# Hash-masked attention and a two-layer block on one core: a new hand-written order for the first two chunks, and a new place for the value shares

## The chip, the core and the metric

The kernel runs on one core of a Trainium2 chip. Times are device microseconds of one launch of the whole program. The kernel before takes 311.88 us (median of 3 runs, 311.78 to 311.99). A core has five instruction streams that run side by side and wait for each other through semaphores: PE (TensorE, matrix products, with a separate row PEld for weight loads), DVE (VectorE), ACT (ScalarE), POOL (GpSimd) and SP, which here only issues DMAs. Each stream runs its instructions in the order in which the program emitted them, so an instruction that waits holds up all that stand behind it on the same engine.

## The reference

Four batches, 8 heads, 768 positions, head size 64. Queries and keys are hashed to six bits each, a query attends only to keys of its own bucket, and the result goes through a normalised two-layer block with a residual:

```
q_bits = einsum('bhsd,dk->bhsk', q, proj) > 0        # six bits; k_bits likewise
mask   = q_bucket[:, :, :, None] == k_bucket[:, :, None, :]
scores = where(mask, scale * q @ k.T, -1e9)
attn   = softmax(scores)                              # plus 1e-9 in the denominator
x      = (attn @ v).transpose(0, 2, 1, 3).reshape(B, S, H * D)
xn     = (x - mean) / sqrt(var + 1e-6) * g_ln
out    = x + relu(xn @ w_ch1) @ w_ch2                 # 512 -> 2048 -> 512
```

## The kernel before

**Tiling.** The work is cut into 12 chunks of 256 query positions, (batch, third) in order: chunks 0 to 2 are batch 0, chunks 3 to 5 batch 1, and so on. A chunk's attention has 12 units: four pairs of heads, three groups of four key blocks for each pair. `att_units` gives four steps for each unit: `scores` (S, four products into a tile `sc`, two buffers), `exps` (X, one 128x1024 exponential on ACT), `values` (V, eight products into an accumulator `av`) and `divide` (D, after the third group of a pair). The mask is part of the scores' product: six rows of plus or minus one half, one for each hash bit, lie below the 64 rows of each head in the operand tiles `slots`. The accumulator `av` lies in one of two PSUM banks, av0 and av1; chunk 0 uses av0 only, other chunks alternate from pair to pair.

**The block.** `mlp_steps` gives for each chunk the normalisation, eight `up` steps (eight products of 128x256 each into `hp`, then a rectifying copy R by DVE or ACT) and eight `down` steps (four products of 128x512 each). The block of one chunk runs as filler between the attention units of the next.

**Operands.** For batches 1 to 3, the operands are made by POOL casts (`narrow`, N), a DMA transpose issued by SP (`operands`, T), a DMA that shifts every second block (`shifted`, P), DVE block transposes (B), hash products (H), a store of the bits to DRAM and four loads of them as rows (J). For batch 0 this would take too long, so `first_two` builds them on the engines: TensorE transposes of the f32 tiles into a PSUM tile `tpose` (T, or LT for the late thirds), a scaled copy to SBUF (`scaled`, E), casts of its upper and lower half into `slots` (`cast`, C), hash products (H, LH), the comparison that writes the bits (`compare`, B) and a copy of the bits for the second row of blocks (`odd_bits`, O). The letter behind a word of the list names the engine: a for ACT, d for DVE, g for POOL. All transposes of before use bank av1, and every copy E of it frees the bank for the next.

**Values.** `values` (vc for batch 0, first half of part V after) casts the v tile. For the later batches part V then runs `value_sums`: five POOL additions whose last writes `self.vs16`, a new tile of a pool with one buffer, for each half of the heads. Part E is `share(half)`: one product of the constant `epsk` with `self.vs16` into the av bank that the running pair doesn't use, and a DVE copy into `vs[half]`. `divide` adds `vs` to `av` for batches 1 to 3. `share` reads the attribute `self.vs16` as it stands when the part is emitted.

**What sets the order.** Chunks 0 and 1 and the first unit of chunk 2 follow the list `opening`, one word for each step; K words are products that only keep PE awake. From chunk 2 on, `interleave` emits for unit u: S and X of unit u+1, fillers up to the share (2u+1)/24 of their summed costs, the square sums (`single`) of odd units, V and D of unit u, and fillers up to (2u+2)/24. The fillers of a chunk are the words of `steps[n]`, in order: d and u cost 870 and 900, H costs 1300, E 110, x 600 and the others nothing.

**Loads.** Batch 0's q and k come in five and five DMAs from SP and ACT, its v in two. POOL issues, at the words w0 to w3, the first weights, q and k of batch 1's first half, the second weights, and q, k of the second half with v of the first. Batch 1's second half of v (W11) is issued by SP, which runs its DMAs in the program's order.

Of the kernel before, what the change touches and what calls it, by code (L numbers as in the profile page):

```python
# [9 lines left out]
F32 = mybir.dt.float32  # L10
# [12 lines left out]
HALF_SCALE = 2.0**-6  # L23
# [7 lines left out]
def kernel(  # L31
# [36 lines left out]
    proj1 = consts.tile([P, D], F32)  # L68
    nc.vector.memset(proj1, 0.0)
    identf = consts.tile([P, P], F32)  # L70
    make_identity(nc, identf)
    nc.gpsimd.dma_start(out=proj1[0:D, 0:n_bits], in_=proj)
# [91 lines left out]
    class Prep:  # L164


        def __init__(self, b):
            self.b, self.tiles = b, {}
            self.sl, self.va, self.vs = slots[b % 2], vaug[b % 2], vsum[b % 2]
            self.qkT, self.nat16, self.bt = {}, {}, {}  # L170

        def load(self, half):
            self.tiles.setdefault(half, {}).update(load_half(self.b, half))
# [16 lines left out]

            return self.sl.rearrange("p h a (c t) -> p h (a c) t", t=P)

        def transposes(self, key):

            tp = ps_av.tile([P, 4, P], F32, tag="av1", name="tpose")
            late = isinstance(key, tuple)
            for g in range(4):
                if late:
                    h, nm, c = 2 * key[1] + g // 2, "q", 2 + 2 * (g % 2)
                else:  # L200
                    h, nm, c = key, "kkkq"[g], 2 * (g % 3)
                nc.tensor.transpose(  # L202
                    tp[:, g, :],
                    self.tiles[h // 4][nm][:, h % 4, c : c + 2].rearrange("p c d -> p (c d)"),
                    identf,
                )
            self.bt[key] = tp

        def scaled(self, key, engine):

# [30 lines left out]

        def cast(self, key, par, engine):

            self.copy_by(
                engine,
                self.places(key, slice(0, D), par),
                self.as_placed(key, self.qkT[key][par * D : (par + 1) * D]),
            )

        def hash_two(self, keys):  # L250

# [25 lines left out]

        def narrow(self, half, a):

            if a == 0:  # L280
# [70 lines left out]
        def values(self, half):  # L351
            hs = slice(half * H // 2, (half + 1) * H // 2)
            nc.gpsimd.tensor_copy(self.va[:, hs, :, 0:D], self.tiles[half]["v"])  # L353
# [65 lines left out]
    def att_units(b, t, x):  # L419
# [15 lines left out]
        for j in range(NP):  # L435
# [7 lines left out]
            for g, grp in enumerate(groups):  # L443
# [18 lines left out]
                    )  # L462
                    state[g] = ex

                def values(grp=grp, g=g, state=state, j=j, ha=ha):
# [14 lines left out]
                    av = state["av"]  # L480
                    for i, (h, kj) in enumerate(grp):
                        for qi in range(TT):
                            nc.tensor.matmul(  # L483
                                av[:, h - ha, qi, :],
                                state[g][:, i, qi * P : (qi + 1) * P],
                                va[:, h, kj, :],
                                start=(b > 0 and (g, i, qi) == (0, 0, 0)),
                                stop=(g == 2 and i == 3),
                                skip_group_check=True,
                            )  # L490
# [27 lines left out]
    def mlp_steps(b, t, x):  # L518
# [53 lines left out]
                        tp[:, dt, i * P : (i + 1) * P], st["xn"][:, dt, i, :], ident  # L572
                    )

        def xcopy():

            st["xnT"] = work.tile([P, ND, CT], BF16, tag="xnT", bufs=1, name="xnT")
            nc.vector.tensor_copy(st["xnT"], st["tp"])  # L578

        def up_products(n2, wide=False):  # L580
            if n2 == 0:
# [119 lines left out]
        )  # L701


    def interleave(units, fillers, after=None, single=()):

# [33 lines left out]
    def chunk_tile():  # L739
# [4 lines left out]
    mlp = {0: mlp_steps(*chunks[0], xs[0])}  # L744

    opening = """
        K26 T0 E0a C0.0a C0.1d K6 T1 E1a C1.1a C1.0d K10 J0 H0 K10 T2 B0 E2a B1 O0a K8 T3 C2.0g
        O1d S0 E3a C2.1d vc0 w0 S1 X0 C3.1d H1 C3.0d X1 su0 B2 T4 sd0 S2 O2a E4a B3 S3 V0 X2
        C4.0g O3d T5 C4.1d V1 w1 E5a V2 S4 X3 C5.0d H2 C5.1d vc1 D2 X4 LT2 B4 S5 LE2a su1 B5 O4g
        X5 T6 O5g sd1 S6 V3 LC2.1g E6a LC2.0d S7 X6 C6.1d C6.0g T7 V4 w2 E7d V5 X7 S8 C7.0d H3  # L750
        C7.1d X8 D5 LT0 B6 V6 LE0a V7 B7 O6g LT1 O7d LC0.0g S9 LE1d LC0.1g V8 S10 X9 LC1.1d LH0
        w3 D8 X10 LC1.0d S11 LB0 V9 X11 V10 LO0d LT3 LB1 S12 LE3a V11 LO1d S13 X12 LC3.0g D11
        LH1 n0 LC3.1g X13 S14 V12 X14 V13 n1 S15 X15 V14 S16 LB2 xt0 nr0 X16 D14 V15 xe0 S17
        LO2g V16 LB3 X17 U0 LO3d S18 R0d U1 na0 X18 bl3 S19 U2 R1a bl0 X19 S20 R2d U3 na1 op0
        bl1 V17 S21 R3a D17 V18 X20 U4 bl2 V19 X21 U5 R4d S22 R5a V20 S23 X22 D20 V21 U6 X23 V22
        S24 R6d V23 X24 U7 D23 R7a
    """

    def first_two():
# [9 lines left out]
        engines = {"a": nc.scalar, "d": nc.vector, "g": nc.gpsimd}  # L769

        def keep_awake(n):
            tp = ps_mm.tile([P, P], F32, tag="mm", name="wakep")
# [19 lines left out]
        def both(i):  # L792
# [2 lines left out]
        table = {  # L795
            "K": lambda n: keep_awake(n),
            "J": lambda n: first_head_projection(),
            "T": lambda h: prep.transposes(h),
            "E": lambda h, e: prep.scaled(h, e),
            "C": lambda h, par, e: prep.cast(h, par, e),  # L800
            "H": lambda j: prep.hash_two([2 * j, 2 * j + 1]),
            "B": lambda h: prep.compare(h),
            "O": lambda h, e: prep.odd_bits(h, e),
            "LT": lambda j: prep.transposes(("late", j)),
            "LE": lambda j, e: prep.scaled(("late", j), e),
            "LC": lambda j, par, e: prep.cast(("late", j), par, e),
            "LH": lambda i: prep.hash_two(both(i)),
# [4 lines left out]
            "V": lambda u: every[u][2](),  # L812
# [5 lines left out]
            "n": lambda i: (parts["stats"](i), parts["centred"](i)),  # L818
            "nr": lambda _: parts["scale"](),
            "xt": lambda _: parts["xt"](),  # L820
            "xe": lambda _: parts["xe"](),
# [4 lines left out]
            "op": lambda _: (nxt.operands(0), nxt.shifted(0)),  # L826
        }
        for word in opening.split():
            name = word.rstrip("0123456789.adg") if word[-1] in "adg" else word.rstrip("0123456789.")
            rest = word[len(name) :]  # L830
            engine = [engines[rest[-1]]] if rest[-1] in engines else []
            numbers = [int(x) for x in rest.rstrip("adg").split(".")]
            table[name](*numbers, *engine)

    steps = {
# [9 lines left out]
    }  # L848
# [41 lines left out]
    for n in range(2, len(chunks)):  # L890
# [11 lines left out]
        if len(single) > 4:  # L902
            single[3:] = [sum(single[3:], [])]
        with tc.manual_schedule():
            interleave(units[n], fillers, after, single)
# [219 lines left out]
```

## Time and profile before

| what | value |
|---|---|
| median of three runs | 311.88 us (311.78 to 311.99) |
| the profiled execution's own time | 311.64 us |
| its span | 309.8 us |
| PE, PEld | 300.2 us (97%), 226.1 us (73%) |
| ACT, DVE, POOL | 217.1 us (70%), 187.1 us (60%), 83.9 us (27%) |
| first `up` products start | 39.44 us |
| last `up` of chunk 0 starts | 50.59 us |

A line of the timeline gives the start in us, the duration in us, the engine, the line of the kernel, the operation, and what is written and read with its shape; a bracket at its end gives the engine's idle time just before and what ended it. SPq and POOLq are the engines' instruction queues, where DMAs are issued. A group line gives busy time, the mean duration in ns, and the idle time before with what ended it. PEclk is the clock granted to TensorE, 1.00 being full. A DMA share above 1.00 counts overlapping packets. Idle time of an engine that sets no end costs nothing.

### The profile page before, as it was taken

To read this page: it belongs to the slowest core of one execution; us is meant where nothing else is said; L and a number is where in the kernel's file an instruction comes from. 1 tells how busy PE (TensorE), PEld (TensorE's weight loads), DVE (VectorE), ACT (ScalarE), POOL (GpSimd) and SP (SyncE) were. 2 spreads that over 40 slices of the span, in tenths; PEclk is the share of its full clock that TensorE was granted. 3 is DMA by queue.
4 is the path that set the end of the run, shared out by engine and by line. 5 is a ranking of instruction groups with operands and counts; after the bars stand their busy time and mean duration, and the time that the engine had idled before them with its cause. 6 is when DMAs were issued, how large, how long until landed. Compare 5 with 4: busy or idle time off the path is not lost.

```text
span 309.8 us, 7840 instructions
## 1 busy us (share of the span) xinstructions
PE 300.2 (97%) x3268; PEld 226.1 (73%) x3268; DVE 187.1 (60%) x404; ACT 217.1 (70%) x272; POOL 83.9 (27%) x110
## 2 busy tenths in 40 slices
PE   6979999999999999999999999999999999999994
PEld 6556788678679679678679669669679678687573
DVE  1799996654756756743783785654743735735522
ACT  5677977776688778678788778778788677666020
POOL 3467540913421127160280470100100100100200
PEclk9999999999999999999999999999999999999998
DMA  7999998377396476695098646131030210200302
GB/s 226 376 210 302 212 331 149 101 123 190 51 323 147 93 247 125 161 301 145 12 263 146 178 89 155 24 71 37 5 98 0 41 65 0 70 36 0 105 0 76
DMA packets 64968, 40.92 MB, mean 132 GB/s; under 512 B 47152, under 2 KB 59952, under 8 KB 64928
## 3 DMA queue, kind: packets, MB, share of 16 engines
q1 hardware_dynamic: 60224, 31.59, 40.5%
q0 software_dynamic: 4128, 8.13, 11.1%
q10 hardware_dynamic: 576, 0.66, 0.6%
q8 instruction: 27, 0.44, 0.6%
q14 instruction: 13, 0.11, 0.1%
HBM read 27.98 MB, written 6.88 MB: 113 GB/s over the span
## 4 chain that ended last, share of the span: by engine, by line
PE 90%; DVE 6%; ACT 2%; issue 1%; POOL 0%; POOLq 0%
PE hp L589 27%; PE o L630 25%; PE sc L448 18%; PE av L483 11%; PE hash L323 3%; DVE slots L264 2%; PE tpose L202 1%; DVE slots L240 1%; PE wakep L774 1%; PE o L612 1%; PE hash L254 1%; ACT qkT L219 1%; DVE x L510 1%; DVE xn L535 0%; DVE stats L529 0%
## 5 line engine op out<-in xcount | busy, mean ns | idle before, releaser
L458 ACT ACTIVATE ex<-sc,expb 128x1024 bf16<-128x1024 f32 x144 | 159.3, 1112 | 55.8 <-PE sc L448 53.1
L589 PE MATMUL hp<-xnT,w_sb 128*128 128x256 bf16 x768 | 98.4, 272 | 0.3 <-DVE xnT L578 0.3
L630 PE MATMUL o<-w_sb,hbuf 128*128 128x512 bf16 x368 | 92.9, 379 | 0.0
L448 PE MATMUL sc<-slots 70*128 70x256 bf16 x576 | 86.5, 272 | 2.0 <-POOL slots L240 1.5
L589 PEld LDWEIGHTS <-w_sb 128*128 128x128 bf16 x768 | 71.9, 98 | 8.9 <-DMA xnT<-xn 0.5
L483 PEld LDWEIGHTS <-ex 128*128 128x128 bf16 x1152 | 54.0, 98 | 15.8 <-ACT ex L458 1.6
L448 PEld LDWEIGHTS <-slots 70*128 70x128 bf16 x576 | 52.0, 97 | 17.6 <-issue 3.7
L483 PE MATMUL av<-vaug,ex 128*128 128x65 bf16 x1152 | 58.8, 194 | 0.5 <-ACT ex L458 0.2
L599 DVE TENSOR_SCALAR hbuf<-hp 128x512 bf16<-128x512 f32 x48 | 33.0, 688 | 42.3 <-PE hp L589 41.2
L630 PEld LDWEIGHTS <-hbuf 128*128 128x128 bf16 x368 | 33.6, 97 | 25.4
L546 POOL TENSOR_SCALAR rs<-mv 128x2 f32<-128x2 f32 x12 | 9.1, 756 | 156.8 <-DVE mv L530 156.8
L601 ACT ACTIVATE hbuf<-hp 128x512 bf16<-128x512 f32 x48 | 28.5, 593 | 19.6 <-PE hp L589 19.6
L635 DVE SCALAR_TENSOR_TENSOR x<-o,rs,x 128x512 f32<-128x512 f32 x23 | 17.1, 744 | 21.9 <-PE o L630 21.9
L510 DVE TENSOR_TENSOR x<-av,rc 128x256 f32<-128x256 f32 x48 | 20.4, 424 | 1.6
L535 DVE SCALAR_TENSOR_TENSOR xn<-x,mv,gbc 128x512 bf16<-128x512 f32 x24 | 17.9, 750 | 0.8
L503 DVE TENSOR_SCALAR rc<-av 128x4 f32<-128x4 f32 x36 | 5.7, 158 | 20.5 <-PE av L483 20.5
L529 DVE BATCH_NORM_STATS2 stats<-x 128x6 f32<-128x512 f32 x24 | 16.5, 690 | 0.4
L504 DVE TENSOR_TENSOR av<-av,vsum 128x256 f32<-128x256 f32 x36 | 15.6, 433 | 1.2
L353 POOL CAST vaug<-vnat 128x1536 bf16<-128x1536 f32 x8 | 11.8, 1470 | 14.1 <-DMA vnat<-in_v_dram 14.1
L182 ACT ACTIVATE knat<-knat 128x768 f32<-128x768 f32 x16 | 13.4, 835 | 0.0
L182 ACT ACTIVATE qnat<-qnat 128x768 f32<-128x768 f32 x16 | 13.3, 833 | 0.0
L284 POOL CAST nat<-qnat 128x1536 bf16<-128x1536 f32 x6 | 8.8, 1469 | 15.9 <-DMA qnat<-in_q_dram 8.1
(85 smaller groups left out, 210.7 us busy)
## 6 DMA issues: line engine op xcount, KB each, us to landing
out_dram<-x SPq DMA_DIRECT2D x23, 256.0 KB
vnat<-in_v_dram SPq DMA_DIRECT2D x7, 768.0 KB
qnat<-in_q_dram SPq DMA_DIRECT2D x11, 384.0 KB
knat<-in_k_dram SPq DMA_DIRECT2D x11, 384.0 KB
w_sb<-in_moe_w_ch_dram POOLq DMA_DIRECT2D x4, 1024.0 KB, 14.5
slots<-slots SPq DMA_DIRECT2D x6, 384.0 KB
qnat<-in_q_dram POOLq DMA_DIRECT2D x2, 768.0 KB, 15.0
knat<-in_k_dram POOLq DMA_DIRECT2D x2, 768.0 KB, 16.2
```

The source lines that it names most:

```text
L182: nc.scalar.activation(src, src, AF.Square, accum_out=sq[:, a, col : col + 1],)
L448: nc.tensor.matmul(sc[:, i, :], key_block(h, kj), query_blocks(h),)
L458: nc.scalar.activation(ex, sc, AF.Exp, bias=expb[:, 1:2] if b else expb[:, 0:1], scale=scale if b else scale / Q_SCALE,)
L483: nc.tensor.matmul(av[:, h - ha, qi, :], state[g][:, i, qi * P : (qi + 1) * P], va[:, h, kj, :], start=(b > 0 and (g, i, qi) == (0, 0, 0)) ...
L510: nc.vector.tensor_tensor(xv, num, rc.unsqueeze(3).to_broadcast([P, 2, TT, D]), op=AOP.mult)
L529: nc.vector.bn_stats(stats, x[:, i, :])
L535: nc.vector.scalar_tensor_tensor(xn[:, :, i, :], x[:, i, :].rearrange("p (o d) -> p o d", d=P), mv[:, i, 0:1], gbc.rearrange("p (o d) -> p ...
L589: nc.tensor.matmul(hp[:, i, :], w1_sb[:, dt, nt * P : (nt + 1) * P], st["xnT"][:, dt, :], start=(dt == 0), stop=(dt == ND - 1),)
L599: nc.vector.tensor_scalar_max(dst, src, 0.0)
L601: nc.scalar.activation(dst, src, AF.Relu)
L630: nc.tensor.matmul(o2, st["h"][:, nt, i * P : (i + 1) * P], w2_sb[:, nt, :], start=(nt == 0), stop=(nt == NH - 1),)
L635: nc.vector.scalar_tensor_tensor(x[:, i, :], o2, st["rs"][:, i : i + 1], x[:, i, :], op0=AOP.mult, op1=AOP.add,)
```

## The change

The change has these parts.

1. The tile `proj1`, its clearing and its load are emitted ahead of all other constants; before, POOL issued the load behind the making of the identity.
2. `transposes` takes a bank: a word such as T1d or LT1d writes the tile in av0 and a word without the letter in av1.
3. A cast by DVE reads the transposes' PSUM tile, with the scaling, and no longer the scaled SBUF copy. The letter p names DVE as well.
4. The list `opening` is new: only the first K word is left (26 of 60 wake products), most E steps go from ACT to DVE, most casts C and bit copies O from DVE to POOL, and the words w0 to w3, the normalisation (its statistics n and its centring ns are now separate words) and all S, X, V, U, R stand in new places. A word Vnd lets a pair of chunk 0 use av1.
5. The shares E leave the filler lists. `interleave` emits them at given units, after `single` and before that unit's V: E10 at unit 10 of chunk 2, E11 at unit 1 of chunk 3, E20 and E21 at units 7 and 10 of chunk 5, E30 and E31 at unit 1 of chunks 7 and 8.
6. `xcopy` can run on ACT (not used by the list), and `narrow` makes its tile for whichever of q and k comes first.

```diff
+    proj1 = consts.tile([P, D], F32)
+    with tc.manual_schedule():
+        nc.vector.memset(proj1, 0.0)
+        nc.gpsimd.dma_start(out=proj1[0:D, 0:n_bits], in_=proj)
+    tc.no_sync_barrier()
...
-        def transposes(self, key):
+        def transposes(self, key, bank=None):
-            tp = ps_av.tile([P, 4, P], F32, tag="av1", name="tpose")
+            tp = ps_av.tile([P, 4, P], F32, tag="av0" if bank else "av1", name="tpose")
...
         def cast(self, key, par, engine):
+            dst, rows = self.places(key, slice(0, D), par), slice(par * D, (par + 1) * D)
+            if engine is nc.vector:
+                nc.vector.tensor_scalar_mul(
+                    dst, self.as_placed(key, self.tp[key][rows]), HALF_SCALE
+                )
+            else:
+                self.copy_by(engine, dst, self.as_placed(key, self.qkT[key][rows]))
...
-                        slot = 0 if (b, t) == (0, 0) else j % 2
+                        slot = (0 if (b, t) == (0, 0) else j % 2) ^ other
...
             if u % 2 and u // 2 < len(single):
                 for _, f in single[u // 2]:
                     f()
+            if u in early:
+                for _, f in prepare(early[u]):
+                    f()
             values()
...
     opening = """
-        K26 T0 E0a C0.0a C0.1d K6 T1 E1a C1.1a C1.0d K10 J0 H0 K10 T2 B0 E2a B1 O0a K8 T3 C2.0g
-        O1d S0 E3a C2.1d vc0 w0 S1 X0 C3.1d H1 C3.0d X1 su0 B2 T4 sd0 S2 O2a E4a B3 S3 V0 X2
...
+        K26 T0 E0d T1d C0.1g E1a J0 C0.0p C1.1g H0 T2 C1.0g E2a T3d B0 O0g B1 E3d C2.0a S0 C3.0p X0
+        O1g LT0 C2.1g vc0 C3.1g S1 H1 X1 S2 LE0d T5d T4 B2 X2 O2g su0 E4a B3 w0 E5d S3 C4.0a sd0 T6d
+        H2 E6d B4 C5.0a V0 C4.1a T7 O3g S4 V1 C5.1g E7d X3 O4a V2 X4 S5 vc1 H3 C7.1p B5 D2 V3d S6 X5
...
-        2: "n d d H10 d d x N11 J10 d N11 B11 d T11 B11 V10 d B11 W11 d B11 u P11 u H11 u J11 E10 u V11 u u u u",
-        3: "n L20 d d d d W20 d E11 d N20 d N20 B20 d T20 u B20 u u B20 u u B20 P20 u u u",
+        2: "n d d H10 d d x N11 J10 d N11 B11 d T11 B11 V10 d B11 W11 d B11 u P11 u H11 u J11 u V11 u u u u",
+        3: "n L20 d d d d W20 d d N20 d N20 B20 d T20 u B20 u u B20 u u B20 P20 u u u",
...
+    shares = {2: {10: "E10"}, 3: {1: "E11"}, 5: {7: "E20", 10: "E21"}, 7: {1: "E30"}, 8: {1: "E31"}}
```

More of the change, by code (lines that the diff above doesn't have):

```diff
@@ L169, in __init__ @@
             self.sl, self.va, self.vs = slots[b % 2], vaug[b % 2], vsum[b % 2]
-            self.qkT, self.nat16, self.bt = {}, {}, {}
+            self.qkT, self.nat16, self.bt, self.tp = {}, {}, {}, {}
         def load(self, half):
@@ L206, in transposes @@
                 )
[L207 removed]
+            self.bt[key] = self.tp[key] = tp
         def scaled(self, key, engine):
@@ L278, in narrow @@
         def narrow(self, half, a):
-            if a == 0:
+            if half not in self.nat16:
                 self.nat16[half] = work.tile(
@@ L463, in exps, with values @@
                     state[g] = ex
-                def values(grp=grp, g=g, state=state, j=j, ha=ha):
+                def values(other=False, grp=grp, g=g, state=state, j=j, ha=ha):
                     if g == 0:
-                        slot = 0 if (b, t) == (0, 0) else j % 2
+                        slot = (0 if (b, t) == (0, 0) else j % 2) ^ other
                         av = ps_av.tile([P, 2, TT, D1], F32, tag=f"av{slot}", name="av")
@@ L573, in xtrans, with xcopy @@
                     )
-        def xcopy():
+        def xcopy(engine=nc.vector):
             st["xnT"] = work.tile([P, ND, CT], BF16, tag="xnT", bufs=1, name="xnT")
-            nc.vector.tensor_copy(st["xnT"], st["tp"])
+            if engine is nc.scalar:
+                nc.scalar.activation(st["xnT"], st["tp"], AF.Copy)
+            else:
+                nc.vector.tensor_copy(st["xnT"], st["tp"])
         def up_products(n2, wide=False):
@@ L701, in safety, with interleave @@
         )
-    def interleave(units, fillers, after=None, single=()):
+    def interleave(units, fillers, after=None, single=(), early=()):
         total = sum(c for c, _ in fillers) or 1
@@ L768, in first_two @@
         parts = mlp[0][4]
-        engines = {"a": nc.scalar, "d": nc.vector, "g": nc.gpsimd}
+        engines = {"a": nc.scalar, "d": nc.vector, "g": nc.gpsimd, "p": nc.vector}
         def keep_awake(n):
@@ L797, in first_two @@
             "J": lambda n: first_head_projection(),
-            "T": lambda h: prep.transposes(h),
+            "T": lambda h, bank=None: prep.transposes(h, bank),
             "E": lambda h, e: prep.scaled(h, e),
@@ L811, in first_two @@
             "X": lambda u: every[u][1](),
-            "V": lambda u: every[u][2](),
+            "V": lambda u, bank=None: every[u][2](bank is not None),
             "D": lambda u: every[u][3](),
@@ L828, in first_two @@
         for word in opening.split():
-            name = word.rstrip("0123456789.adg") if word[-1] in "adg" else word.rstrip("0123456789.")
+            name = word.rstrip("0123456789.adgp") if word[-1] in engines else word.rstrip("0123456789.")
             rest = word[len(name) :]
             engine = [engines[rest[-1]]] if rest[-1] in engines else []
-            numbers = [int(x) for x in rest.rstrip("adg").split(".")]
+            numbers = [int(x) for x in rest.rstrip("adgp").split(".")]
             table[name](*numbers, *engine)
     steps = {
[2 rows of a table removed]
[2 rows of a table added]
         4: "n L21 d d d H20 d J20 d d N21 d N21 B21 d T21 V20 u B21 u u B21 u u B21 P21 W21 u u u",
[1 row of a table removed]
[1 row of a table added]
         6: "n L31 d d d N30 d N30 B30 d T30 B30 d B30 d B30 d P30 V30 u u u u W31 u u u u",
[2 rows of a table removed]
[2 rows of a table added]
         10: "n d d d d m d d d d u u u s u u u u u",
@@ L904 @@
         with tc.manual_schedule():
-            interleave(units[n], fillers, after, single)
+            interleave(units[n], fillers, after, single, shares.get(n, {}))
     tc.no_sync_barrier()
```

29 lines of the change are left out of this document (10 added, 19 removed), and 6 rows, old and new, of the table steps.

## The prediction

> **What bounds the kernel now.** I read the page first, for the engine that carries the span, then the chain that ended last.
>
> ```profile
> PE 300.2 (97%) x3268; PEld 226.1 (73%) x3268; DVE 187.1 (60%) x404; ACT 217.1 (70%) x272; POOL 83.9 (27%) x110
> PE 90%; DVE 6%; ACT 2%; issue 1%; POOL 0%; POOLq 0%
> ```
>
> PE is the bound. In the stretches after 50 us it is busy in 49.8 to 50.0 of each 50 us, so there only PE work or a new PE wait changes the time. The rest of the chain lies in the first 40 us. There I read the timeline and the groups up to 52 us:
>
> ```profile
> 9.74 0.60 ACT L219 ACTIVATE qkT<-tpose 128x512 f32<-128x512 f32 x1 [2.31 <-PE tpose L202]
> 10.39 0.31 PEld L202 LDWEIGHTS tpose<-identf,knat 128*128 128x128 f32 x3 [0.41 <-ACT qkT L219]
> ...
> 22.40 0.60 PE L448 MATMUL sc<-slots 70*128 70x256 bf16 x4 [1.50 <-POOL slots L240]
> ...
> 39.44 1.03 PE L589 MATMUL hp<-xnT,w_sb 128*128 128x256 bf16 x8 [0.30 <-DVE xnT L578]
> ```
>
> ```profile
> L264 DVE TENSOR_SCALAR slots<-hash 38x512 bf16<-38x512 f32 x12 | 8.3, 688 | 1.5 <-PE hash L254 1.2
> L240 DVE CAST slots<-qkT 64x512 bf16<-64x512 f32 x10 | 6.1, 611 | 6.3 <-ACT qkT L219 6.1
> L240 DVE CAST slots<-spare 64x512 bf16<-64x512 f32 x4 | 3.9, 984 | 0.5 <-ACT spare L219 0.4
> ```
>
> The reader sees one bank handed round between PE and ACT (T, then E 0.60, then the next T), scores that wait 1.50 us for bit copies, and DVE casts that take 0.41 alone and up to 2.43 us beside POOL casts.
>
> Last, the stretch into which the first share moves, with the DMA queue's and POOL's rows beside PE's:
>
> ```profile
> 53.93 0.73 SPq L314 DMA_DIRECT2D slots<-slots  x1
> ...
> 60.37 3.15 SPq L342 DMA_DIRECT2D slots<-bits_d  x4
> 63.57 3.77 SPq L306 DMA_TRANSPOSE slots<-nat  x1
> 67.45 0.52 SPq L157 DMA_DIRECT2D vnat<-in_v_dram  x1
> ...
> 74.27 1.47 POOL L353 CAST vaug<-vnat 128x1536 bf16<-128x1536 f32 x1 [10.70 <-DMA vnat<-in_v_dram]
> 75.07 0.40 PEld L483 LDWEIGHTS <-ex 128*128 128x128 bf16 x8
> ...
> 78.71 0.66 POOL L362 TENSOR_TENSOR vs<-vsum,vaug 128x256 bf16<-128x256 f32 x1
> ```
>
> The values of batch 1's second half are asked for at 67.45, land at 74.2, and their sum is ready at 79.37.
>
> **The opening, part by part.** The load of `proj` moves from 1.54 to about 0.95 on POOL (after the DVE clearing, 0.11); its landing took 5.5 us, so 7.04 becomes 6.45, between 0 and 0.6 earlier. The 34 wake products that go took 0.43, 0.65, 0.56 and 0.54 of PE (2.2 us), partly in time that PE waited anyway. Two banks let the next T start 0.4 after the last instead of 1.35 (9.04 to 10.39). ACT loses 7 of its 10 copies E (7 x 0.60 = 4.2 us) and gains one cast on balance (0.63). DVE loses 14 casts and 6 bit copies (6.1 + 3.9 + 2.3 = 12.3 us) and gains 7 copies E at 0.69 (row L221) and 4 casts from PSUM. No row shows that cast: its ends are 0.41 (the shortest cast from SBUF) and 0.69 (L221 and L264, both from PSUM); I take 0.69, the same source: 11 x 0.69 = 7.6. POOL gains 8 casts at 0.65 and 7 bit copies at 0.61 (9.5 us).
>
> I walked the new order by hand with these durations, S 0.43, V 0.34, U 0.87, H 1.0 and X 1.09 apart, and 0.05 between engines. Landing times bound it: SP's eight small `proj` loads wait in turn for the loads of batch 0, and their issues (9.31, 10.59, 11.64, 12.69, 13.77, 14.82, 16.87) date the landings. T0 at 4.2, T1 at 5.2, first hash 6.7 (7.51 before), T2 and T3 at 8.5 and 8.9 (9.04, 10.39), first exponential 10.5 (11.74), T5 not before k of heads 4 and 5 at 12.7, T6 not before 14.85, sixth S6 20.2 (22.40), S12 27.9 (32.48), first `up` 35.9 (39.44), and the list ends at 48.0 instead of 51.65: 3.65 us earlier. Its ends: 0, and 5.1 if PE never waited after T2 (38.0 us of PE work from 8.5). The square sums, `narrow`'s guard and the idle ACT branch of `xcopy` cost nothing: same instructions.
>
> POOL's DMA words come later: w0 12.65 to 13.4, w1 16.29 to 23.6, w2 24.4 to 26.6, w3 30.0 to 36.3. They are covered, because the queue they feed drains one after the other (210 GB/s until 26, 390 until 30, 210 until 41, 390 until 47.5 in the windows of 1 us): each still comes before its forerunner has drained. If w1 came 2 us later still, that cover would be gone and all that follows in the DMA would move by as much.
>
> **The share at unit 10 of chunk 2.** Its filler list puts V11 behind 13760 of 17360 cost units (0.79), which falls due in unit 9. So V11 is emitted ahead of E10, and E10's product now reads the sum that V11 writes, that of the other half: the built order has it so, with a wait on POOL. The product stands on PE between the seventh `up` step and the V that began at 75.07; all of chunk 3 is queued behind it.
>
> When is that sum ready? Its v load is SP's 28th step, behind the first transpose (T10), the shift, the bit store, an output store, four bit rows and the second transpose. The step that decides is the shift, which waits for T10. DMA was full until T10's packets ended:
>
> ```profile
> 51.00:52.00 1.00, 1.00 (x11) 0.89 (x10) 0.96 (x2) 1.00 (x2) 0.00 (x0) 1.00 1.21 275
> 52.00:53.00 1.00, 1.00 (x10) 0.51 (x9) 0.93 (x3) 1.00 (x2) 0.00 (x0) 1.00 0.00 0
> ```
>
> The last two columns are DMA share and GB/s. The amount to be moved is the same, so T10 ends at 52 again however early PE is; POOL's two casts ahead of it end at 41.5 in my walk (41.96). The shift moves 55.4 to 58.7 and the bit rows follow at 60.4, as before, then the transpose and the v load. So the sum is ready at 79.4 again, and PE, there at 75.05 - 3.65 = 71.4, waits 8 us. Against before: 79.37 + 0.05 (semaphore) + 0.11 (share) - 75.07 = +4.46. The opening's gain lies wholly inside this wait. Bounds for the ready time: 78.4 (no dip in the loads at 5.5 to 6.5 us, where 143 and 231 GB/s stand between 357 and 372, and the bits stored sooner) to 80.9 (w1 or w3 leaves a gap).
>
> **The clock after the wait.** At the end of the trace PE's last matmul ends at 305.8:
>
> ```profile
> 305.50:306.00 0.50, 0.29 (x3) 0.01 (x1) 0.17 (x1) 0.00 (x0) 0.00 (x0) 1.00 0.68 234
> 307.50:308.00 0.50, 0.00 (x0) 0.00 (x0) 0.00 (x0) 0.00 (x0) 0.00 (x0) 1.00 0.32 96
> 308.00:308.50 0.50, 0.00 (x0) 0.00 (x0) 0.00 (x0) 0.00 (x0) 0.00 (x0) 0.50 0.04 12
> ```
>
> The third column from the right is the granted clock: half after 2.2 us of idleness. The wait of 8 us is longer. Coming back costs what it costs at the start: the 26 first wake products took 2.69 us of weight loads where later ones take 0.057 each (1.48), so 1.2 us, or 1.7 if the slow time lasts until 4.5. I take +1.5, ends 0 and 2.
>
> [...]
>
> **The other shares.** Before, PE waited 0.2 at E11 (85.31) and 0.43 at E21 (143.83 to 144.26); mid-pair the bank is free, so -0.6 (0 to -0.9). E20 in chunk 5 also reads the later half's sum: that was ready at 138.35, the product's new place is 139.8, so 1.4 us to spare.
>
> **Sum**, against the profiled execution's 311.64 (0.24 below the median): 311.64 + 4.46 + 1.5 - 0.6 = 317.0, and 317.2 beside the median. By the bounds 314.9 to 319.3.
>
> **The rivals.**
> - The chain moves with PE. If the bit rows had waited for the output store (59.69 on SP, tied to PE), the sum would come 3.65 earlier: 311.64 + 0.8 + 1.5 - 0.6 = 313.3. Against it: SP had 0.34 us to spare behind that store, and waited on.
> - Faster: PE doesn't wait, because the sum stands when PE comes. Then the opening counts: 311.64 - 3.65 - 0.8 = 307.2. The place is the same product; for all of it the sum must be ready by 71.4, that is a v load landed by 66.3, before it was even issued in this trace, and below the time of before it falls from a sum ready by about 74.0 (75.07 - 0.16 - 1.5 + 0.6). For it: only a queue quite unlike this one.
> - The opening stalls instead, on POOL's 9.5 us more (POOL at 85% from 6 to 39 us). Up to 4 us of that would vanish in the wait too; the time stays near 317.
> - The two halves cancel: a sum 3.5 us sooner and a PE warm at once give 311.64 + 0.96 - 0.6 = 312.0. It needs both at a time.
>
> **How the numbers follow.** Forecast 0.74, chain moving with PE 0.10, faster 0.12, cancelling 0.04. No change is within 0.2% (0.6 us). The likeliest case alone is 314.9 to 319.3; leaving the faster and the cancelling case and a thin tail out, the range is 313.0 to 319.5.
>
> **What would show it.** After: the first share's PE row with an idle time of some 8 us ended by POOL's `vs` addition, near 79.4; granted clock 0.5 in the windows around it; first `up` near 36; no wait at E20. The prediction is wrong if that v load is issued well ahead of 67 us, or if the share's row shows no wait.

## The result, and the profile after

| | before | after |
|---|---|---|
| median | 311.95 us (311.78 to 312.2, 5 runs) | 315.56 us (314.81 to 316.35, 5 runs) |
| profiled execution | 311.64 us, span 309.8 | 316.35 us, span 314.6 |
| mean granted clock, profiled | 0.997 | 0.984 |

The changed kernel is slower by 1.2%: ratio 1.0118, 95% interval 1.0096 to 1.014, which is +3.6 us by the medians and +4.7 between the two profiled executions. One execution in this record, 313.64 us at a clock of 0.983 in the last experiment, was in a slower state of the chip and is left out of that experiment's median.

From the page of after: the engines' busy time, the granted clock in 40 slices, and the chain that ended last.

```profile
PE 298.6 (95%) x3207; PEld 225.3 (72%) x3234; DVE 181.8 (58%) x395; ACT 213.6 (68%) x266; POOL 91.9 (29%) x125
PEclk9999999996699999999999999999999999999999
PE 85%; DMA 7%; SPq 2%; DVE 2%; POOL 2%; issue 1%; DVEq 0%
PE hp L596 26%; PE o L637 24%; PE sc L452 18%; PE av L487 11%; DMA knat<-in_k_dram 3%; PE hash L327 2%; DMA vnat<-in_v_dram 2%; DMA bits_d<-bits 1%; SPq L310 1%; PE tpose L204 1%; PE o L619 1%; DMA qnat<-in_q_dram 1%; PE hash L258 1%; SPq L346 1%; POOL vsum L366 1%
```

PE's work hardly changed (300.2 to 298.6 us), but its share fell from 97% to 95%, and two slices, around 71 to 86 us, have a clock of 0.6. PE's part of the chain fell from 90% to 85%, and DMA, which had no share in it, has 7%. By the last line, 4 of these 7 are the first loads of q and k, for which the opening now waits. What is new behind the opening is a v load, a store of bits, SP's transpose and POOL's sums, and they lead up to the slow slices.

The timeline of after at that place, for SP, POOL, PEld and PE:

```profile
60.48 3.14 SPq L346 DMA_DIRECT2D slots<-bits_d  x4
63.67 3.80 SPq L310 DMA_TRANSPOSE slots<-nat  x1
67.58 0.52 SPq L159 DMA_DIRECT2D vnat<-in_v_dram  x1
...
71.09 0.69 SPq L318 DMA_DIRECT2D slots<-slots  x1
...
72.95 1.47 POOL L357 CAST vaug<-vnat 128x1536 bf16<-128x1536 f32 x1 [10.05 <-DMA vnat<-in_v_dram]
77.39 0.65 POOL L366 TENSOR_TENSOR vs<-vsum,vaug 128x256 bf16<-128x256 f32 x1
...
70.43 0.10 PEld L371 LDWEIGHTS <-epsk 128*128 128x128 bf16 x1
78.09 0.37 PE L371 MATMUL share<-vs,epsk 128*128 128x256 bf16 x1 [7.39 <-POOL vs L366]
78.71 1.90 PE L596 MATMUL hp<-xnT,w_sb 128*128 128x256 bf16 x8
```

PE loads the share's weights at 70.43 and then stands still for 7.39 us until POOL's last addition, which makes the sum of the other half of the heads. That sum hangs on a v load issued at 67.58, practically where it was before (67.45). By the code the value changes with it: in batches 1 and 2, `vs` of the first half is made from the sum of the second, and a query with no key in its bucket takes its result from `vs` alone. The first eight `up` products behind the wait take 1.90 us; the last eight ahead of it, at a clock of 1.00, took 1.04.

Windows of the same stretch (columns: stretch, its length, busy time and instructions of PE, PEld, DVE, ACT and POOL, granted clock, DMA share, GB/s):

```profile
72.00:73.00 1.00, 0.00 (x0) 0.00 (x0) 0.00 (x0) 0.00 (x0) 0.04 (x1) 1.00 1.05 369
73.00:74.00 1.00, 0.00 (x0) 0.00 (x0) 0.00 (x0) 0.00 (x0) 1.00 (x1) 0.73 0.88 194
74.00:80.00 6.00, 1.91 (x16) 1.45 (x16) 0.42 (x1) 0.00 (x0) 3.64 (x6) 0.50 0.29 52
80.00:83.00 3.00, 3.00 (x16) 2.07 (x15) 0.69 (x1) 1.11 (x1) 0.00 (x0) 0.50 0.06 6
83.00:84.00 1.00, 1.00 (x14) 0.90 (x13) 0.32 (x2) 0.60 (x1) 0.00 (x0) 0.65 0.00 0
```

The clock falls inside the wait and is still at half for 5.6 us after PE has begun again.

So the account of the profiled execution, by marks that both kernels have: the weight load of the V behind the share moves from 75.07 to 78.09 (+3.0), the first `down` products in chunk 3 from 78.31 to 83.99 (+5.7), and the last group of PE products from 302.14 to 307.18 (+5.0). The wait's end gives 3.0, the slow clock 2.7, and what follows gives 0.6 back. The span behind the last group is 0.2 shorter (7.66 to 7.42), and so +4.8 in all.

The opening did what it was written for. From the timeline of after:

```profile
8.51 0.52 PE L204 MATMUL tpose<-identf,knat 128*128 128x128 f32 x3 [0.97 <-DMA knat<-in_k_dram]
9.41 0.60 PE L452 MATMUL sc<-slots 70*128 70x256 bf16 x4
...
35.49 1.91 PE L596 MATMUL hp<-xnT,w_sb 128*128 128x256 bf16 x16
```

The first `up` stands at 35.49 instead of 39.44, and PE is at the share 4.6 us earlier than before. All of it lies inside the wait.

### The profile page after: what moved, and what is told of

The parts are those of the page before. It is cut to its first block, busy times and chain, and to the rows that moved or that the text cites. A ratio compares the mean times of both kernels' runs of the same rounds, so it can differ in the third digit from the quotient of the medians.

```text
span 314.6 us, 7751 instructions
## 1 busy us (share of the span) xinstructions
PE 298.6 (95%) x3207; PEld 225.3 (72%) x3234; DVE 181.8 (58%) x395; ACT 213.6 (68%) x266; POOL 91.9 (29%) x125
## 4 chain that ended last, share of the span: by engine, by line
PE 85%; DMA 7%; SPq 2%; DVE 2%; POOL 2%; issue 1%; DVEq 0%
PE hp L596 26%; PE o L637 24%; PE sc L452 18%; PE av L487 11%; DMA knat<-in_k_dram 3%; PE hash L327 2%; DMA vnat<-in_v_dram 2%; DMA bits_d<-bits 1%; SPq L310 1%; PE tpose L204 1%; PE o L619 1%; DMA qnat<-in_q_dram 1%; PE hash L258 1%; SPq L346 1%; POOL vsum L366 1%
## 5 line engine op out<-in xcount | busy, mean ns | idle before, releaser
L462 ACT ACTIVATE ex<-sc,expb 128x1024 bf16<-128x1024 f32 x144 | 159.2, 1112 | 64.5 <-PE sc L452 62.2
L596 PE MATMUL hp<-xnT,w_sb 128*128 128x256 bf16 x768 | 100.1, 276 | 0.0
L637 PE MATMUL o<-w_sb,hbuf 128*128 128x512 bf16 x341 | 90.0, 379 | 1.3
```

The lines of the kernel that those rows point to most:

```text
L462: nc.scalar.activation(ex, sc, AF.Exp, bias=expb[:, 1:2] if b else expb[:, 0:1], scale=scale if b else scale / Q_SCALE,)
L596: nc.tensor.matmul(hp[:, i, :], w1_sb[:, dt, nt * P : (nt + 1) * P], st["xnT"][:, dt, :], start=(dt == 0), stop=(dt == ND - 1),)
L637: nc.tensor.matmul(o2, st["h"][:, nt, i * P : (i + 1) * P], w2_sb[:, nt, :], start=(nt == 0), stop=(nt == NH - 1),)
```

## Experiments

The theory on record: the share at its new place is a product of the sum that V11 makes, PE waits for that sum, the sum's date is set by SP's queue and not by PE, and so the opening's gain is hidden. The rivals: it is the new opening, or the share's new place as such, that costs the time. In the table, "mark" is the start of the last group of PE products in the profiled execution (302.14 before, 307.18 after); it leaves out what comes behind PE's work. Each ratio is to runs of the kernel before that were made beside it; their medians lie between 311.82 and 312.25, so medians of different rows compare only to some tenths of a microsecond.

| kernel | median us | ratio to before, 95% | mark, against before |
|---|---|---|---|
| after | 315.56 | 1.0118 (1.0096 to 1.014) | +5.04 |
| after, sums kept by half | 309.0 | 0.9905 (0.9885 to 0.9926) | -3.57 |
| old opening, new shares | 316.86 | 1.0147 (1.0116 to 1.0179) | +5.50 |
| old opening, new shares, sums by half | 311.31 | 0.9968 (0.9955 to 0.9981) | -0.15 |
| after, wake products in the wait | 313.97 | 1.0058 (1.0032 to 1.0083) | +3.27 |
| sums by half, second share later | 307.37 | 0.9854 (0.9837 to 0.987) | -5.17 |
| new opening, old shares | 307.17 | 0.9845 (0.983 to 0.986) | -4.54 |
| after, v load first | 306.68 | 0.9826 (0.9798 to 0.9854) | -4.91 |
| sums by half, v load first | 308.03 | 0.9878 (0.9852 to 0.9905) | -4.95 |
| new opening, old shares, casts from SBUF | 306.81 | 0.9824 (0.9798 to 0.9849) | -4.25 |
| the same, one bank for T1 and T3 | 308.11 | 0.9896 (0.9852 to 0.9941) | -3.30 |

### Each half's sum kept by half

```diff
-            self.vs16 = work.tile([P, H // 2, D], BF16, tag="vs16", bufs=1, name="vs16")
+            vs16 = self.vs16[half] = work.tile([P, H // 2, D], BF16, tag="vs16", bufs=2, name="vs16")
...
-            nc.tensor.matmul(ps, epsk, self.vs16.rearrange("p h d -> p (h d)"))
+            nc.tensor.matmul(ps, epsk, self.vs16[half].rearrange("p h d -> p (h d)"))
```

> The kernel after, with one thing changed: each half's value sum is kept under its half, so that the first share reads the sum of its own half, which is ready long before. Theory (one wait on PE, and the slow clock behind it, cost all): PE came to the first share at 70.4 where the kernel before came to the V behind it at 75.07, so 4.6 us are gained by then, and 0.9 more by the later shares (offset 5.7 us at the first down step of chunk 3, 4.8 at the end). So 311.95 - 4.6 - 0.9 = 306.4, between 305.8 and 307.3, no idle time at the first share, granted clock 1.00 throughout. Rival (the new opening or the new places cost time by themselves, through POOL's longer queue or the DMA): 311 or more.

Measured: 309.0 us (308.87 to 309.89). The first share stands at 70.53 with no wait and the clock stays at 1.00 (in all windows up to 300), so the cause is the sum that the product reads, and not the place of the product. But 306.4 was missed by 2.6 us. Timeline of this kernel, at the second share (unit 1 of chunk 3):

```profile
70.53 0.27 PE L372 MATMUL share<-vs,epsk 128*128 128x256 bf16 x1
...
77.62 0.99 POOL L367 TENSOR_TENSOR vs<-vsum,vaug 128x256 bf16<-128x256 f32 x1
78.66 0.27 PE L372 MATMUL share<-vs,epsk 128*128 128x256 bf16 x1 [1.45 <-POOL vs L367]
```

The second half's sum still comes at 78.6. PE, now 4.6 us earlier, meets it at the next product that needs it, and stands for 1.45 us there. I had not looked at that product. A further 1.0 us of the profiled execution lies behind PE's work: DVE's last row ends at 302.74 and the span at 307.2, 4.46 us later, against 3.49 before and 3.24 after. Three later experiments come back to both.

### The old opening with the new shares

The opening of before, with the shares at the new places and one sum tile, as in after.

```diff
-        2: "n d d H10 d d x N11 J10 d N11 B11 d T11 B11 V10 d B11 W11 d B11 u P11 u H11 u J11 E10 u V11 u u u u",
+        2: "n d d H10 d d x N11 J10 d N11 B11 d T11 B11 V10 d B11 W11 d B11 u P11 u H11 u J11 u V11 u u u u",
...
+    shares = {2: {10: "E10"}, 3: {1: "E11"}, 5: {7: "E20", 10: "E21"}, 7: {1: "E30"}, 8: {1: "E31"}}
```

> The kernel before, its opening untouched, with only the shares moved to the places of the kernel after (the first share reads the later half's sum here too). Theory: PE comes to the first share at 75.0 and waits for the same sum, ready at 78.0 to 79.4, so the time is that of the kernel after or up to 2.6 us more: 311.95 + 3.0 to 4.5 + 2.6 (clock) - 0.9, 315.6 to 318.2, with a wait of 3 to 4.4 us in place of 7.4. Rival (the parts add up, and the opening saves 4.6 us in both): 315.6 + 4.6 = 320.2. If the clock does not fall in so short a wait, 313 to 315.5.

Measured: 316.86 us (315.7 to 317.78), within the theory's range and far from the 320.2 of two costs that add up. The shares alone make the loss, and with the old opening PE waits less, because it comes later:

```profile
78.87 0.65 POOL L362 TENSOR_TENSOR vs<-vsum,vaug 128x256 bf16<-128x256 f32 x1
79.57 0.27 PE L367 MATMUL share<-vs,epsk 128*128 128x256 bf16 x1 [4.14 <-POOL vs L362]
```

4.14 us here, 7.39 with the new opening: the difference, 3.25, and the wait's end, 1.5 later here (79.57 to 78.09), make up the 4.6 that the opening gains, to within 0.2. Windows of this kernel show the clock:

```profile
76.00:79.00 3.00, 0.00 (x0) 0.00 (x0) 0.00 (x0) 0.25 (x1) 2.69 (x5) 1.00 0.04 6
80.00:80.50 0.50, 0.50 (x8) 0.44 (x5) 0.31 (x1) 0.00 (x0) 0.00 (x0) 0.88 0.25 23
80.50:83.50 3.00, 3.00 (x16) 2.06 (x14) 0.69 (x1) 1.11 (x1) 0.00 (x0) 0.50 0.10 9
```

It was full through the whole wait and fell 0.8 us after PE had begun again.

### The old opening, new shares, each sum kept by half

The last kernel with the first experiment's edit. It shows what the new places are worth when nothing waits.

```diff
-            nc.tensor.matmul(ps, epsk, self.vs16.rearrange("p h d -> p (h d)"))
+            nc.tensor.matmul(ps, epsk, self.vs16[half].rearrange("p h d -> p (h d)"))
```

> The kernel before, its opening untouched, with the shares at their new places, and each share reading the sum of its own half. Theory: only the waits at the old places go, 0.2 at E11 and 0.43 at E21 and some 0.2 at E10: 311.95 - 0.9 = 311.1, between 310.8 and 311.5. Rival (the old places cost nothing, since the DVE copies only move): 311.95.

Measured: 311.31 us (310.64 to 311.68) beside 312.18 for before, in the expected range: the places themselves are worth about 0.3% (interval 0.2% to 0.45%).

### Wake products in the wait

Ahead of the first share's product, 116 products of constants into the same bank, which that product then overwrites.

```diff
             ps = ps_av.tile([P, H // 2 * D], F32, tag=f"av{1 - pair_bank[-1]}", name="share")
+            if (self.b, half) == (1, 0):
+                for _ in range(116):
+                    nc.tensor.matmul(ps[:, 0:P], wake, wake)
```

> The kernel after, with 116 wake products on PE ahead of the first share, into the share's own bank: they fill about 6.6 of the 7.4 us of the wait, and the wait's end stays with the sum. Theory: the clock stays at 1.00, and the 5.3 us at half clock behind the wait (78.1 to 83.4) go, 2.65 us: 315.6 - 2.65 = 312.9, between 312.3 and 313.6, and the runs scatter no more than those of the kernel before. Rival (the clock's fall does not reach the end, since other engines set the pace after the wait): 315.6.

Measured: 313.97 us (313.22 to 316.04), 1.6 us less than after where 2.65 was expected. That is above the range of 312.3 to 313.6, and the runs scatter by 2.8 us where those of the kernel before scatter by 1.7. Timeline of this kernel:

```profile
71.09 6.64 PE L373 MATMUL share<-wake 128*128 128x128 bf16 x116
78.69 0.27 PE L374 MATMUL share<-vs,epsk 128*128 128x256 bf16 x1 [0.95 <-POOL vs L366]
79.04 1.04 PE L599 MATMUL hp<-xnT,w_sb 128*128 128x256 bf16 x8
```

The clock is 1.00 in all windows from 69 to 85, and the products behind the share take 1.04 again instead of 1.90. The wait itself ends when it ended (0.6 later in this profile, with the sum). So the slow clock is a term of its own, but its size is less sure. The 2.65 was that of one execution: in the four other runs of after the mean clock was 0.989 and not 0.984, so by that mean they had less time at half clock (last section). And the 1.6 may be too small, by what a later sum took back: in this one profile that is 0.6, and by the marks 1.8 + 0.6 = 2.4 us stand against the 2.65.

### The second share later

The first experiment's kernel, with E11 at unit 4 of chunk 3.

```diff
-    shares = {2: {10: "E10"}, 3: {1: "E11"}, 5: {7: "E20", 10: "E21"}, 7: {1: "E30"}, 8: {1: "E31"}}
+    shares = {2: {10: "E10"}, 3: {4: "E11"}, 5: {7: "E20", 10: "E21"}, 7: {1: "E30"}, 8: {1: "E31"}}
```

> The changed kernel with each half's sum kept by half, and the second half's share (E11) moved from unit 1 of chunk 3 to unit 4, some 4 us later on PE. Theory (the sum of the second half is made once, near 78.6, and whatever product comes before it stands on PE until then): no PE row of a share shows an idle time, the granted clock stays 1.00, and the 1.7 us that the second share cost with the sums kept apart go: 309.0 - 1.7 = 307.3 (306.6 to 307.9). Rival (the second share was only the first place at which a PE ahead of ACT's exponentials was stopped, and the next wait takes its place): 308.6 to 309.2, with PE's idle time moved to an S or V row behind it.

Measured: 307.37 us (307.08 to 307.98), as the theory had it: no share waits, and no other wait takes the place.

### The new opening with the old shares

After's opening, with the filler lists of before, which hold the E words.

```diff
-    shares = {2: {10: "E10"}, 3: {1: "E11"}, 5: {7: "E20", 10: "E21"}, 7: {1: "E30"}, 8: {1: "E31"}}
+    shares = {}
```

> The changed kernel's opening with the shares back at their old places between the d and u steps. Theory (the opening is worth some 4.6 us at the first share, and the shares' new place alone brings the wait of 7.4): the first share reads its own half's sum, so PE does not wait for it; the sum of the second half still comes near 78.6, and E11 stood at 85.3 before, now near 80.7, so without a wait or with one below 0.5: 311.95 - 4.6 + 0 to 0.5 = 307.6 (307.0 to 308.5). Rival (the opening's gain is lost again behind the opening, on ACT's exponentials or on transfers that keep their old dates, whatever the shares do): 309.5 to 311.5. A third (the opening is itself no gain, and only the first share's earlier arrival looked like one): 311.5 to 312.5.

Measured: 307.17 us (306.79 to 307.4), the theory's 307.6 and neither rival. The opening alone is worth 4.65 us, by the mark 4.54, and it lasts to the end. As built, this is the one part of the change that pays.

### The v load ahead of the bit rows

After itself. The words V10, W11 and J10 change places in the list, but every engine's order stays as it was except SP's, where the v load goes ahead of the rows and the transpose. It keeps after's reading of the second half's sum in the first share.

```diff
-        2: "n d d H10 d d x N11 J10 d N11 B11 d T11 B11 V10 d B11 W11 d B11 u P11 u H11 u J11 u V11 u u u u",
+        2: "n d d H10 d d x N11 d N11 V10 W11 J10 B11 d T11 B11 d B11 d B11 u P11 u H11 u J11 u V11 u u u u",
```

> The changed kernel, in which the v load of the second half is issued ahead of the bit rows and the second transpose on SP, instead of behind them; nothing else moves on any engine. Theory (the first share waits for the sum of the second half, and that sum's date is the place of the v load in SP's queue): the load is issued at 59.4, as soon as POOL's cast of the first half's values (57.79 to 59.3) frees the tile, lands near 64.7, the sum is ready near 69.9, and PE, at the share at 70.43, does not wait; the clock stays 1.00 and the wait of 7.4 and the slow time of 2.65 go together: 306.9 (306.0 to 308.0). If the load takes 9 us beside the output store, the sum comes at 74, PE waits 3.6 and the time is 310 to 311. Rival (the wait is that of the share's new place, for its bank or for another engine, and the sum only ends last): 314.5 to 316.5, with PE's idle time before the share ended by something else. Rival 2 (bit rows and transpose come late and chunk 3's scores wait): a PE idle time on an S row after 80, 308 to 312.

Measured: 306.68 us (305.96 to 307.57), 8.9 below after by medians of two sessions. Timeline of this kernel:

```profile
59.05 0.39 SPq L159 DMA_DIRECT2D vnat<-in_v_dram  x1
59.93 3.49 SPq L346 DMA_DIRECT2D slots<-bits_d  x4
63.47 4.43 SPq L310 DMA_TRANSPOSE slots<-nat  x1
...
64.53 1.47 POOL L357 CAST vaug<-vnat 128x1536 bf16<-128x1536 f32 x1 [1.86 <-DMA vnat<-in_v_dram]
68.96 0.65 POOL L366 TENSOR_TENSOR vs<-vsum,vaug 128x256 bf16<-128x256 f32 x1
...
70.33 0.27 PE L371 MATMUL share<-vs,epsk 128*128 128x256 bf16 x1
70.69 1.04 PE L596 MATMUL hp<-xnT,w_sb 128*128 128x256 bf16 x8
```

The load is issued 8.5 us earlier, the sum stands at 69.61, PE comes at 70.33 and goes on, and the clock stays at 1.00 (windows from 68 to 85). The bit rows and the transpose behind it begin no later than they began (60.48 and 63.67 in after), because the rows were waiting for the stored bits anyway: SP's wait for them was 2.2 us in after and is 0.5 here. That settles the cause: the first share needs the second half's sum, and the date of that sum is the place of one DMA in SP's queue. The value is still that of the other half, so this kernel shows the cause and isn't one to keep; those with the sums by half and those with the old shares have the right sum.

### Both: sums by half, and the v load first

The edit of the kernel above, made to that of the first experiment.

```diff
-        2: "n d d H10 d d x N11 J10 d N11 B11 d T11 B11 V10 d B11 W11 d B11 u P11 u H11 u J11 u V11 u u u u",
+        2: "n d d H10 d d x N11 d N11 V10 W11 J10 B11 d T11 B11 d B11 d B11 u P11 u H11 u J11 u V11 u u u u",
```

> The changed kernel with each half's sum kept by half (as in the first experiment) and the v load ahead of the bit rows and the transpose on SP. Theory (the 1.5 us at the second share, unit 1 of chunk 3, were the same sum that came at 78.6): the sum stands near 69.7, so neither share waits (the second comes near 76.9), and the time is 309.0 - 1.7 = 307.3, by PE's own rows 306.6 to 307.3; range 306.0 to 308.0. Rival (the second share's wait was made by POOL's additions being drawn out beside other work, whenever they come): a wait of 0.5 to 1.5 stays at the second share, 308 to 309.

Measured: 308.03 us (307.4 to 309.79), just above the range of 306.0 to 308.0 and, by the time alone, at the rival's lower end of 308. The rival's sign, a wait at the second share, is absent. Timeline of this kernel:

```profile
68.86 0.65 POOL L367 TENSOR_TENSOR vs<-vsum,vaug 128x256 bf16<-128x256 f32 x1
70.17 0.27 PE L372 MATMUL share<-vs,epsk 128*128 128x256 bf16 x1
...
76.68 0.27 PE L372 MATMUL share<-vs,epsk 128*128 128x256 bf16 x1
```

Neither share waits, the sum stands at 69.5, and POOL's three additions ahead of the last take 2.12 us, to 2.11 in after, where they took 2.44 in the first experiment. So the second share's wait was for the same late sum, as the theory said. PE's mark, 297.19, is that of the kernel above (297.23). In the profiles the rest is behind PE: 4.43 us from DVE's last row to the end, to 3.39 there. The three kernels with the new opening and sums by half all have this 1.0 us more in their profiles; the one with the old opening has not (3.2). In the windows of 0.4 us it is one more small DMA piece, over 2 us after the output's last large one, and no instruction of the timeline stands beside it. What makes it stays open.

### Casts from SBUF

The new opening with the old shares, in which DVE's four casts read the scaled copy, as in before.

```diff
-            if engine is nc.vector:
-                nc.vector.tensor_scalar_mul(
-                    dst, self.as_placed(key, self.tp[key][rows]), HALF_SCALE
-                )
-            else:
-                self.copy_by(engine, dst, self.as_placed(key, self.qkT[key][rows]))
+            self.copy_by(engine, dst, self.as_placed(key, self.qkT[key][rows]))
```

> The new opening with the shares at their old places, in which VectorE's four bit casts of q and k read the copy E in SBUF, as in the kernel before, instead of PSUM. Theory (the cast from PSUM costs 0.68 to the 0.41 of the shortest from SBUF, and DVE has room in the opening): within 0.3 of the same kernel with casts from PSUM, 306.9 to 307.5, the row of the four casts at 0.41 to 0.5. Rival (casts from SBUF are drawn out where POOL casts beside them, up to 2.43 in the kernel before, and the first scores wait for them): 307.6 to 308.7, the row's mean over 0.8.

Measured: 306.81 us (306.36 to 307.59), to 307.17 with casts from PSUM: no difference that can be told. The row was forecast at 0.41 to 0.5 and has 0.54. The four casts, by group, in this kernel and then in the one with casts from PSUM:

```profile
L242 DVE CAST slots<-qkT 64x512 bf16<-64x512 f32 x4 | 2.2, 542 | 0.1
```

```profile
L248 DVE TENSOR_SCALAR slots<-tpose 64x512 bf16<-64x512 f32 x4 | 2.7, 683 | 0.1
```

From PSUM they take 0.68 each, the price that was taken. The part "VectorE's casts from PSUM" neither pays nor costs an amount that these runs could show.

### One bank for the first transposes

The last kernel, with T1 and T3 in the bank of T0 and T2. Casts from PSUM read T0's bank behind T1, which one bank doesn't allow; hence the base with casts from SBUF.

```diff
-        K26 T0 E0d T1d C0.1g E1a J0 C0.0p C1.1g H0 T2 C1.0g E2a T3d B0 O0g B1 E3d C2.0a S0 C3.0p X0
+        K26 T0 E0d T1 C0.1g E1a J0 C0.0p C1.1g H0 T2 C1.0g E2a T3 B0 O0g B1 E3d C2.0a S0 C3.0p X0
```

> The same as the one with casts from SBUF, and the transposes T1 and T3 in the one bank of T0 and T2, as in the kernel before. Theory (one bank makes T1 wait for the copy E0 and T3 for E2, and PE does not get it back): T3 starts near 9.6 instead of 8.73, and the time is 0.7 (0.3 to 1.2) over that with two banks. Rival (PE waits for k's landing at T5 and for hash bits anyway, so it is absorbed): 0 to 0.2 over it.

Measured: 308.11 us (307.63 to 311.58 in five runs). The runs scatter too much for the median; the profiled executions differ by 0.8 us (308.11 to 307.33) and the marks by 0.95, both within the forecast. Timeline of this kernel:

```profile
6.25 0.55 PE L204 MATMUL tpose<-identf,knat 128*128 128x128 f32 x3 [0.79 <-DVE qkT L223]
9.95 0.55 PE L204 MATMUL tpose<-identf,knat 128*128 128x128 f32 x3 [0.69 <-ACT qkT L221]
```

T1 and T3 wait 0.79 and 0.69 for the copy that frees the bank, and PE gets only part of it back. By one profiled execution of each kernel, the second bank at these two places is worth about 0.9 of the opening's 4.6. The rest of the 4.6 (fewer wake products, the exchange of engines, the earlier `proj`, the new order) was not taken apart.

## Why the prediction was right, and what was mis-sized

The forecast, 317.2, stands 1.6 above the median and its sum for a profiled execution, 317.0, 0.65 above the one measured. The mechanism was right: the product reads the other half's sum, PE waits for it on POOL, the opening's gain went into the wait, and the clock fell. The sum's date was to stay, and moved 1.3 us while PE moved 4.6. That the sum of the terms lies so near the profiled execution is in part luck: the wait's end was 1.4 too late in the forecast and the slow clock 1.2 too short, and the two misses offset each other there.

- **The opening.** Forecast 3.65 us earlier at the share, measured 4.6, within the ends 0 and 5.1. The walk was close up to the first `up` (35.9, measured 35.49) and too cautious behind it: PE is busy in 15.95 of the 16 us from 36 to 52. In the predicted time the term stood at nothing, since the wait covered it, and so its error cost nothing.
- **The sum's date.** This is the larger miss: 79.37 forecast, 78.04 measured, just below the bounds of 78.4 to 80.9. The v load was issued at 67.58, as walked, but landed by 72.9 and not at 74.2. In before, the second shift was issued at 69.18, while the v load was in flight; in after at 71.09. In five kernels that keep the load at its old place in SP's queue the two go together: with the old opening (before, and the old opening with the new shares) the shift is issued 1.7 and 1.8 us behind the load, and POOL's cast starts 6.8 and 6.7 us behind it; with the new one (after, sums by half, wake products) it's 3.5 to 3.6 and 5.4. That doesn't tell the shift from the rest of the opening, and the cause of the faster load stays open. "As before" was right from the bit rows to the load (60.48, 63.67, 67.58 to 60.37, 63.57, 67.45), but not by the stated reason alone. T10 was to end at 52 however early PE is; in after the DMA share is still 1.27 from 53.0 to 53.5 and 0.60 from 53.5 to 54.0, and then 0.01. The shift behind it was issued 0.9 later than before (54.87 to 53.93), the bits' store 1.5 sooner (55.70 to 57.22), and the rows began at the old date. The whole step, forecast +4.46, measured +3.0.
- **The clock.** Forecast +1.5 with ends 0 and 2; in the profiled execution 2.65. By the medians: 315.56 - 306.68 between after and the kernel with the v load first is 8.9, less the wait of 7.4 leaves 1.5; the wake products gave 1.6. The 1.6 may be too small, as said there, so the usual run lies somewhere from 1.5 to 2.4, and the value taken is at the lower end of that. The upper end of 2 was too low for the profiled execution. There the clock was slow until 5.6 us after the restart, while the end of 2 was worked out from the slow products at the start of before, until 4.5 at the longest (26 weight loads in 2.69 us from 1.05 on, 0.10 each; six in 0.43 from 4.52 on, 0.07 each). That those slow products tell what the clock costs behind a wait was my estimate: the windows of before show a clock of 1.00 there, from 0 to 5.
- **The other shares.** Forecast -0.6, measured -0.64 (from +5.68 at chunk 3's `down` to +5.04 at the last group). The kernel with the old opening and sums by half gives the same from its own marks, +0.49 to -0.15. The forecast's 0.43 at E21 was a distance between two starts; the row's idle time there is 0.16. E20 showed no wait, as forecast, with 0.85 us to spare (144.20 to 145.05) for the forecast's 1.4.
- **The sum.** In the profiled execution +3.0 + 2.65 - 0.6 - 0.2 = +4.8, measured +4.7. With 1.5 for the clock it is +3.7, beside +3.6 by the medians; but that 1.5 was itself taken from medians, so this is no second proof. The bounds, stated as 314.9 to 319.3, come out as 314.8 and 319.3 with the other shares held at -0.6; with their own ends they would be 314.5 and 319.9.
- **The rivals.** "The chain moves with PE" falls by SP's rows. "The opening stalls" falls by the opening's marks, and by the experiment with the old shares, in which all 4.6 us arrive. "Faster" named its condition rightly, a sum ready by 71.4, that is a v load landed by 66.3: with the load moved forward on SP it landed by 64.5, and the time was 306.68, where 307.2 was worked out. I held that for possible only in a queue quite unlike this one, but a single DMA moved ahead of four rows and a transpose was enough.
- **POOL's load words and casts.** Taken at nothing, and so it was: w1 at 23.58 and w2 at 26.52 (forecast 23.6 and 26.6), and first `up` not later than walked.

## What to carry to other kernels

When a step moves ahead of another that rebinds a name, a buffer or an attribute, look up which producer it now reads: the product itself costs 0.27 us, the producer's date cost 7.4, and the value that it reads is another one. Before crediting time that is gained ahead of a wait, follow the awaited chain back to the step that doesn't move with the gain; here that was one DMA in SP's queue, and moving it turned a loss of 3.6 us into a gain of 5.6 (306.68 beside 312.25). And when a wait is removed, look at the next product that needs the same late result, because an engine that comes earlier may stand there instead (1.45 us in the first experiment).

## What the runs showed of the hardware that was not expected

The time at half clock behind a wait differed between these runs. In after the granted clock fell at 73.46 and rose at 83.70 (from windows of 0.2 us), 10.24 us at half, with a wait of 7.39. With the old opening and the new shares it fell at 80.38 and rose at 83.80, 3.42 us, with a wait of 4.14. For after the mean agrees: 0.984 over 314.6 us is 10.1 us at half. For its four other runs there is only the mean, 0.989 in each; over 313.5 us that is an estimated 6.9 us at half. A wait's price for the clock was therefore no fixed number in these runs: of 10.24 us at half, 5.6 lay behind the restart, and of the 3.42 all did.

The fall didn't keep a fixed distance from PE's last product: 2.8 us behind it in after (70.70 to 73.46), 5.0 in the other kernel (75.43 to 80.38), the last 0.8 of which PE was at work again.
